# Exponential into two SBUF tiles in turns, token ring one slot shorter

## The chip, the cores and the metric

The kernel runs on one core of a Trainium2 chip. The metric is the time of one execution on the device in microseconds, over all of the kernel's work. Five engines take part, each with its own queue that it works through in order: TensorE (PE in the profile, with its weight loads as PEld), VectorE (DVE), ScalarE (ACT), GpSimd (POOL) and SyncE (SP), which here only issues DMAs. TensorE writes to PSUM alone; VectorE and ScalarE read and write PSUM and SBUF; GpSimd and the DMAs work on SBUF in this kernel.

## The reference

Causal attention with a bias from cumulated positions, and after it a maxout feed-forward on the tokens. There are 8 batches, 8 heads, 576 positions and 64 dimensions a head; the feed-forward goes from 512 to 768 and back to 512.

```python
scores = scale * np.matmul(q, k.transpose(0, 1, 3, 2))
cum = np.cumsum(np.maximum(s, 0.0), axis=-1)
bias = -(cum[:, :, :, None] - cum[:, :, None, :])
scores = np.where(causal, -1000000000.0, scores + np.minimum(bias, 0.0))
scores = scores - np.max(scores, axis=-1, keepdims=True)
attn = np.exp(scores)
attn = attn / (np.sum(attn, axis=-1, keepdims=True) + 1e-09)
x = np.matmul(attn, v)        # then [B, S, H*D] -> [4608, 512]
h = np.maximum(np.maximum(x @ w1, x @ w2), x @ w3)
out = h @ w_out
```

## The kernel before

**Visits and steps.** Heads are worked on in pairs, and a pair's queries in blocks of 128 (the last block has 64). A visit is one pair with some of its blocks. Batches 0 and 1 have two visits a pair, of blocks 0 and 1 and of blocks 2, 3 and 4 (16 visits, 40 steps). Batches 2 to 7 have one visit a pair, of all five blocks: 24 visits, 120 steps, steps 40 to 159. A step is one block for both heads of the pair. Block 0 looks at 128 keys, block 1 at 256, and so on to 512; block 4, with 64 queries of each head stacked on the 128 partitions, looks at all 576. `stacked(v)` (line 118) is true for the visits of five blocks, and `below(t)` (line 114) for their blocks 0 to 3.

**The path of a step.** `scores(t)` (line 362) multiplies on TensorE into a PSUM tile `s` of two banks, one a head; there are two such tiles, in turns. In a visit of five blocks the matmuls are those of lines 379, 390 and 395, and they read two tiles a head, `h` and `l`. `highest(t)` (line 452) masks and takes the smallest of the negated scores on VectorE (line 456), in place in PSUM, with the constant `later` as second input; block 4 has a plain maximum (line 461). `expo(t)` (line 465) takes the exponential on ScalarE with the row sums (line 471), back into the same PSUM tile, and scales the sums (`se`, line 476). `probs(t)` (line 481) takes the reciprocal `ri` (line 494) on VectorE, makes the high half of the probabilities `prh` in 16 bits on ScalarE (line 510), and on VectorE the low half, `prl` = probability minus high half (line 513). Both read the PSUM tile; `prl` reads `prh` as its second input. The halves go through DMA transposes on SyncE's queue (lines 516 and 522) to `ph` and `pl`, which `values` (line 563) multiplies with the values' halves `vh` and `vl` (line 582). `prl` in block 4 has a second instruction of 64 columns; its `prh` counterpart also writes into the tile `prl`.

**The token groups.** `values` gives a slab of tokens `x`, in a high half (ScalarE, line 591) and a low half (VectorE, line 592). The four pairs of a batch and a phase (phase 0: the first 256 positions; phase 1: the other 320) make a set, and `add_set` (line 700) queues its 22 groups: 18 up projections of 12 matmuls (line 714), each evicted by ScalarE (line 728) or VectorE (line 731), with the hidden halves `hh` and `hl` made by GpSimd (lines 720 and 721), and 4 down projections of 18 matmuls (line 756), evicted by ScalarE (line 764) with the scale `os` from GpSimd (line 749). Groups use three PSUM tiles in turns.

**The ring.** The token slabs of the first three pairs of a set's second phase, and of all four pairs of the first phase from batch 2 on, lie in weight tiles that are free by then: `RING` (line 535) names them, and `x_tile` takes the next in turn, 14 times in all. `reserve` (line 537) runs groups of the queue until the set that held that tile has issued its up projections. The tiles `w22` and `w23` hold the last two raw weights; both are decoded by step 17.

**Order.** The schedule is written out by hand: the order of the program is the order on each engine. A step of the loop at line 929 goes

```python
parts = probs(t); next(parts)      # ri, prh
highest(t + 1)
next(parts)                        # prl, transposes
drain(); flush()                   # evictions that are pending, hh and hl
if ready() and cost[0] > 0: run_group()
scores(t + 2)
expo(t + 1)
drain(); flush()
...                                # what the plan has for this step
while ready() and cost[0] > 0: run_group()
values(*due.pop(0))                # where a phase of a visit is complete
```

How many groups run in a step is set by a budget, `cost`: a step earns 4400 ns (4700 from step 60) less what its scores and values cost TensorE, and a group costs 0.417 ns a column and matmul. Among the plan's entries are the preparation of the next visits: the halves of queries and keys (`h` by ScalarE at lines 153 and 157 and by VectorE at line 162, `l` by GpSimd at lines 140 to 146, 166 and 171), the values' halves (ScalarE line 349, VectorE line 354), the decoding of the weights (through tiles with the tag `t`, three of them, line 612) up to step 17, and `later_keys` (line 446) at step 20.

Of the kernel before, what the change touches and what calls it, by code (L numbers as in the profile page):

```python
# [8 lines left out]
F32 = mybir.dt.float32  # L9
F32R = mybir.dt.float32r  # L10
F16 = mybir.dt.float16
BF16 = mybir.dt.bfloat16
I32 = mybir.dt.int32
I64 = mybir.dt.int64
AF = mybir.ActivationFunctionType
# [6 lines left out]
def kernel(  # L22
# [11 lines left out]
    P = 128  # L34
    D = 64
    B, NP, _, QKV = qkv.shape
    HB, S = s.shape
# [8 lines left out]
    Q4 = 4 * P  # L46
# [12 lines left out]
    wpool = ctx.enter_context(tc.tile_pool(name="wpool", bufs=1))  # L59
# [3 lines left out]
    moe = ctx.enter_context(tc.tile_pool(name="moe", bufs=1))  # L63
# [8 lines left out]
    steps = [(v, qb) for v, (_, _, qbs) in enumerate(visits) for qb in qbs]  # L72
# [41 lines left out]
    def below(t):  # L114
        v, qb = steps[t]
        return stacked(v) and qb < 4

    def stacked(v):
        return len(visits[v][2]) == 5
# [65 lines left out]
    def load_w(i, dma=None):  # L185
# [14 lines left out]
        out=tri, in_=tri, pattern=[[-1, P]], compare_op=ALU.is_ge, fill=NEG, base=0, channel_multiplier=1  # L200
    )
    nc.gpsimd.memset(tri4, 0.0)
    for j in range(2):
        r = slice(j * D, (j + 1) * D)
        nc.gpsimd.affine_select(
            out=tri4[r], in_=tri4[r], pattern=[[-1, D]], compare_op=ALU.is_ge, fill=NEG, base=0, channel_multiplier=1
# [153 lines left out]
    U = {}  # L360
# [83 lines left out]
    future = []  # L444

    def later_keys():
        m = wpool.tile([P, Q4], BF16, tag="w23", name="later")
        nc.gpsimd.memset(m[:, 0:Q4 - P], 0.0)
        nc.gpsimd.tensor_copy(out=m[:, Q4 - P:Q4], in_=tri)
        future.append(m)  # L450
# [14 lines left out]
    def expo(t):  # L465
        ps, nm, nk = U[t]
        nj = 2 if nk < S else 1
        sm = small.tile([P, 2], F32, tag="sm", name=f"sm{t}")
        for j in range(nj):
            sc = ps[:, j] if nj == 2 else ps  # L470
            nc.scalar.activation(  # L471
                out=sc, in_=sc, func=AF.Exp, bias=nm[:, j:j + 1], scale=-1.0 if below(t) else 1.0,
                accum_out=sm[:, j:j + 1],
            )
        se = small.tile([P, 2], F32, tag="se", name=f"se{t}")
        nc.scalar.activation(out=se[:, :nj], in_=sm[:, :nj], func=AF.Copy, scale=1.0 / PSC, bias=EPS / PSC)
        SE[t] = (se, nj)
# [54 lines left out]
    taken = [0]  # L532
    done = set()

    RING = [f"w{n}" for n in (10, 11, 12, 13, 14, 15, 16, 17, 22)]

    def reserve(tag, b, ph):
        while owner.get(tag, (b, ph)) not in done | {(b, ph)}:
# [3 lines left out]
    def x_tile(v, ph):  # L542
# [11 lines left out]
        if g == 0:  # L554
            tag = RING[taken[0] % len(RING)]
            taken[0] += 1
# [218 lines left out]
    later = []  # L775
# [85 lines left out]
    for v in range(NP, len(visits)):  # L861
        w = v - NP
# [7 lines left out]
    for f, e in ((prep4, 1), (prep5, 0), (load, 7), (prep2, 4), (prep3, 3)):  # L870
        for v in range(len(visits)):
            t = first[v] - e
            if v % NP == 0 and f in (prep4, prep5):
                t = first[v] + 1 + (f is prep5) if v else -1
# [4 lines left out]
            if f is load and NP <= v < 2 * NP:  # L879
                t = first[v] - 6  # L880
            if 2 * NP * NB - 2 <= v < 2 * NP * NB and f in (load, prep2, prep3):
                t = first[v] - (8 if f is load else 4 if f is prep3 and v % 2 == 0 else 5)
            if stacked(v) and f in (load, prep2, prep3):
                n = v - 2 * NP * NB
# [22 lines left out]
    for i, t in fetched.items():  # L907
        at(t, load_w, i, nc.scalar.dma_start)
    at(1, spread, 1)
    at(20, later_keys)  # L910

    prep2(0)
# [9 lines left out]
    vscale1(scale_of(0))  # L922
    scores(1)
    expo(0)
    for t in sorted(k for k in todo if k < 0):
        for f, a in todo[t]:
            if f not in (prep2, prep3) or a[0] > 1:
                f(*a)
    for t, (v, qb) in enumerate(steps):
# [18 lines left out]
        if t + 1 < len(steps):  # L948
            expo(t + 1)
# [73 lines left out]
```

## Time and profile before

| | |
|---|---|
| three runs | 895.49, 897.57, 898.87 us; median 897.57 |
| profiled execution | span 895.1 us from the first to the last instruction; no other time of it is given |
| TensorE matmuls | busy 818.6 us, 91% of the span |
| VectorE | 599.0 us, 67% |
| ScalarE | 569.4 us, 64% |
| GpSimd | 347.9 us, 39% |
| mean granted TensorE clock | 0.964 |

The profile is of one execution. A row of grouped instructions reads: line, engine, operation, what it writes and reads, shapes, count, then the busy time of the group in us and the mean of one in ns, then the idle time of the engine before them and what ended it. A row of waits reads: engine and what it wrote, what it waited for, then the us in total, how many times, and the longest. In the timeline a row has the start, the duration, the instructions, and in brackets the idle time before. Names of tiles are given without their numbers, so `s` is the scores' tile of any step.

### The profile page before, as it was taken

Reading aid. Unit: us, or ns where it says so; the run is one execution under the profiler, and the core shown is the slowest. Engines: PE = TensorE matmul, PEld = TensorE weight load, DVE = VectorE, ACT = ScalarE, POOL = GpSimd, SP = SyncE. Lnnn points to the kernel's source line nnn. Section 1 sums busy time; section 2 is a strip of 40 time slices with the busy share of each in tenths; the row PEclk is TensorE's granted clock in tenths of the full one; section 3 lists DMA queues with packets and bytes.
Section 4 is the critical chain, followed back from the end, with each engine's and each line's share of the span. In section 5 each row is a group of like instructions: output and inputs, shape, how many; then the busy total and the mean of one; then the engine's idle time right before and its main releaser. Section 6 shows DMA issues by size and latency. Waiting matters only on the chain.

```text
span 895.1 us, 19807 instructions
## 1 busy us (share of the span) xinstructions
PE 818.6 (91%) x7000; PEld 641.1 (72%) x7000; DVE 599.0 (67%) x1504; ACT 569.4 (64%) x1502; POOL 347.9 (39%) x553
## 2 busy tenths in 40 slices
PE   3567769998999989999999999999999999999998
PEld 2445657776667768777787778777787788777875
DVE  6898886666777767676666767676767667663110
ACT  4668567676677677766666776767667676754111
POOL 4111322223444535454454545445454436421211
PEclk9856889999999999999999999999999999999999
DMA  8972446676778676857767676866657777534000
GB/s 297 284 189 60 95 96 142 142 147 141 183 166 174 144 169 127 141 134 147 137 154 159 103 172 141 160 140 139 139 146 147 144 149 129 116 74 85 13 13 30
DMA packets 240243, 122.32 MB, mean 137 GB/s; under 512 B 216016, under 2 KB 224720, under 8 KB 240144
## 3 DMA queue, kind: packets, MB, share of 16 engines
q1 hardware_dynamic: 236112, 108.73, 57.4%
q10 hardware_dynamic: 4032, 12.32, 4.1%
q8 instruction: 55, 0.90, 0.5%
q14 instruction: 44, 0.36, 0.2%
HBM read 60.18 MB, written 9.44 MB: 78 GB/s over the span
## 4 chain that ended last, share of the span: by engine, by line
PE 63%; DVE 3%; ACT 3%; POOL 2%; issue 1%; DMA 1%; SPq 0%; DVEq 0%; POOLq 0%; ACTq 0%
PE pm L714 36%; PE po L756 13%; PE s L379 6%; PE av L582 6%; PE s L390 2%; DVE prl L513 1%; ACT prh L510 1%; ACT s L471 1%; DVE m L731 1%; POOL hh L720 1%; DMA raw<-in_qk_dram 1%; POOL l L171 0%; POOL hl L721 0%; DVE h L162 0%; DVE s L456 0%
## 5 line engine op out<-in xcount | busy, mean ns | idle before, releaser
L714 PE MATMUL pm<-x,w 128*128 128x256 f16 (+1 forms) x3456 | 453.5, 288 | 3.8 <-DVE x L592 2.1
L714 PEld LDWEIGHTS <-w 128*128 128x128 f16 x3456 | 329.7, 98 | 94.4 <-issue 8.4
L720 POOL CAST hh<-m 128x256 f16<-128x256 f32 (+1 forms) x96 | 55.3, 576 | 356.7 <-DVE m L731 299.3
L510 ACT ACTIVATE prh<-s,ri 128x512 f16<-128x512 f32 (+3 forms) x288 | 142.1, 539 | 81.0 <-DVE ri L494 76.4
L513 DVE SCALAR_TENSOR_TENSOR prl<-s,ri,prh 128x512 f16<-128x512 f32 (+3 forms) x288 | 152.9, 568 | 47.4 <-ACT prh L510 29.0
L731 DVE SCALAR_TENSOR_TENSOR m<-pm,m 128x256 f32<-128x256 f32 (+1 forms) x192 | 87.3, 455 | 125.2 <-PE pm L714 100.7
L471 ACT ACTIVATE s<-s,nm 128x512 f32<-128x512 f32 (+4 forms) x288 | 151.2, 525 | 12.6 <-DVE nm L456 5.6
L756 PE MATMUL po<-hh,w 128*128 128x256 f16 (+1 forms) x768 | 149.9, 287 | 0.0
L756 PEld LDWEIGHTS <-w 128*128 128x128 f16 x1152 | 110.1, 98 | 33.4 <-issue 4.8
L456 DVE CUSTOM_DVE_ANT_0 s<-s,later 128x128 f32<-128x128 f32 (+1 forms) x192 | 94.7, 493 | 33.5 <-PE s L379 30.2
L756 PE MATMUL po<-hl,w 128*128 128x320 f16 (+1 forms) x384 | 110.1, 287 | 1.5 <-POOL hl L721 1.4
L728 ACT ACTIVATE m<-pm 128x256 f32<-128x256 f32 (+1 forms) x96 | 39.1, 407 | 93.9 <-PE pm L714 89.5
L721 POOL TENSOR_TENSOR hl<-m,hh 128x256 f16<-128x256 f32 (+1 forms) x96 | 75.4, 785 | 7.8
L171 POOL TENSOR_TENSOR l<-raw,h 64x576 fp32r<-64x576 f32 x48 | 67.2, 1400 | 12.5 <-ACT h L157 11.1
L764 ACT ACTIVATE o<-po,os 128x256 f32<-128x256 f32 (+1 forms) x64 | 31.9, 499 | 62.0 <-PE po L756 53.2
L461 DVE TENSOR_REDUCE nm<-s 128x1 f32<-128x576 f32 (+3 forms) x64 | 49.9, 780 | 22.0 <-PE s L395 12.4
L140 POOL CAST l<-kb 64x576 fp32r<-64x576 f32 x48 | 32.2, 671 | 72.8 <-PE s L390 71.5
L582 PEld LDWEIGHTS <-vh 128*64 128x64 f16 x832 | 45.9, 113 | 19.0 <-issue 13.1
L379 PE MATMUL s<-h 128*128 128x128 f32 (+1 forms) x192 | 54.0, 363 | 4.2 <-DVE prl L513 1.7
L471 ACT ACTIVATION_READ_ACCUMULATOR s<-s,nm 128x1 f32 x288 | 57.3, 199 | 0.0
L591 ACT ACTIVATE x<-av 128x256 f16<-128x256 f32 (+1 forms) x64 | 26.2, 410 | 41.1 <-PE av L582 39.9
L582 PE MATMUL av<-ph,vh 128*64 128x320 f16 (+3 forms) x384 | 51.9, 290 | 0.0
(139 smaller groups left out, 1086.6 us busy)
## 6 DMA issues: line engine op xcount, KB each, us to landing
raw<-in_qk_dram SPq DMA_DIRECT2D x48, 608.0 KB, 4.7
r<-in_w_dram ACTq DMA_DIRECT2D x20, 512.0 KB, 4.9
rv<-in_qkv_dram SPq DMA_DIRECT2D x32, 320.0 KB, 3.3
out_dram<-o SPq DMA_DIRECT2D x32, 160.0 KB, 2.0
out_dram<-o SPq DMA_DIRECT2D x32, 128.0 KB, 2.0
raw<-in_qkv_dram SPq DMA_DIRECT2D x8, 480.0 KB, 3.9
ph<-prh SPq DMA_TRANSPOSE x192, 3.3
pl<-prl SPq DMA_TRANSPOSE x192, 2.9
```

Source lines behind the costliest of these rows:

```text
L171: nc.gpsimd.tensor_tensor(out=l[far, QP:V0], in0=raw[far, QP:V0], in1=h[far, QP:V0].bitcast(F32), op=ALU.subtract)
L379: nc.tensor.matmul(ps[:, j, :nk], lhsT=w[:, qs], rhs=w[:, QP:QP + nk], start=(x == "h"), stop=(x == "l"), skip_group_check=True,)
L456: nc.vector.tensor_tensor_reduce(out=sc[:, j], in0=sc[:, j], in1=future[0][:, Q4 - nk:Q4], scale=-1.0, scalar=3.0e38, op0=ALU.add, op1=ALU ...
L471: nc.scalar.activation(out=sc, in_=sc, func=AF.Exp, bias=nm[:, j:j + 1], scale=-1.0 if below(t) else 1.0, accum_out=sm[:, j:j + 1],)
L510: nc.scalar.activation(out=hi, in_=src, func=AF.Copy, scale=sc)
L513: nc.vector.scalar_tensor_tensor(out=lo, in0=src, scalar=sc, in1=hi, op0=ALU.mult, op1=ALU.subtract)
L582: nc.tensor.matmul(av[j * D:(j + 1) * D, c0:nq], lhsT=lt, rhs=rt, start=(n < 2), stop=(n >= len(todo) - 2), skip_group_check=True,)
L714: nc.tensor.matmul(pm[:, :nq], lhsT=w[:, wt, kt, :], rhs=xt, start=(n == 0), stop=(n == 3 * NKT - 1))
L720: nc.gpsimd.tensor_copy(out=st["hh"][:, ft, :nq], in_=m1[:, :nq])
L721: nc.gpsimd.tensor_tensor(out=st["hl"][:, ft, :nq], in0=m1[:, :nq], in1=st["hh"][:, ft, :nq], op=ALU.subtract)
L731: nc.vector.scalar_tensor_tensor(out=m1[:, :nq], in0=pm[:, :nq], scalar=HSC, in1=m1[:, :nq], op0=ALU.mult, op1=ALU.max)
L756: nc.tensor.matmul(pm[:, :nq], lhsT=W[18 + ft][:, wt, dt, :], rhs=st[ht][:, ft, :nq], start=(n == 0), stop=(n == 3 * NFT - 1),)
```

## The change

In visits of five blocks `expo` writes the exponential to an SBUF tile `e` of 32 bits instead of back to PSUM, in `w22` and `w23` in turns, and `probs` reads it from there. The row sums are taken as before. `w22` leaves the ring, which has eight slots then instead of nine. `later` moves from `w23` to a tile with the tag `t`.

```diff
     def later_keys():
-        m = wpool.tile([P, Q4], BF16, tag="w23", name="later")
+        m = moe.tile([P, Q4], BF16, tag="t", name="later", bufs=3)
@@ expo
         sm = small.tile([P, 2], F32, tag="sm", name=f"sm{t}")
+        e = ps
+        if stacked(steps[t][0]):
+            e = wpool.tile([P, 2 * Q4], F32, tag=f"w{22 + t % 2}", name=f"e{t}")
+            e = e[:, 0:2 * nk].rearrange("p (j n) -> p j n", j=2) if nj == 2 else e[:, 0:S]
+            U[t] = (e, nm, nk)
         for j in range(nj):
-            sc = ps[:, j] if nj == 2 else ps
+            sc, so = (ps[:, j], e[:, j]) if nj == 2 else (ps, e)
             nc.scalar.activation(
-                out=sc, in_=sc, func=AF.Exp, bias=nm[:, j:j + 1], scale=-1.0 if below(t) else 1.0,
+                out=so, in_=sc, func=AF.Exp, bias=nm[:, j:j + 1], scale=-1.0 if below(t) else 1.0,
                 accum_out=sm[:, j:j + 1],
             )
@@
-    RING = [f"w{n}" for n in (10, 11, 12, 13, 14, 15, 16, 17, 22)]
+    RING = [f"w{n}" for n in (10, 11, 12, 13, 14, 15, 16, 17)]
```

## The prediction

> **What bounds the kernel now.** I read the totals first, then the span cut at 250 and 800 us, then TensorE's waits in the middle part.
>
> ```profile
> PE 818.6 (91%) x7000; PEld 641.1 (72%) x7000; DVE 599.0 (67%) x1504; ACT 569.4 (64%) x1502; POOL 347.9 (39%) x553
> ```
>
> ```profile
> core 0: us, PE busy (x) PEld busy (x) DVE busy (x) ACT busy (x) POOL busy (x), PEclk, DMA share, GB/s
> 0.00:250.00 250.00, 189.78 (x1597) 147.36 (x1598) 195.93 (x427) 166.14 (x427) 71.58 (x115) 0.88 0.65 162
> 250.00:800.00 550.00, 537.77 (x4648) 422.74 (x4647) 382.46 (x1029) 382.73 (x1028) 259.60 (x409) 1.00 0.69 143
> 800.00:895.10 95.10, 91.03 (x759) 70.95 (x757) 20.66 (x49) 20.49 (x49) 16.68 (x31) 1.00 0.16 36
> ```
>
> The visits of five query blocks lie in the middle part. There TensorE is busy 537.8 of 550 us at full clock, so 12.2 us is all that an edit of its waiting can win. The first 250 us hold 60 us of idle TensorE, but there `e` is still the PSUM buffer; the last 95 us are token groups. Both stay as they are. In the middle part these waits end TensorE's idle time:
>
> ```profile
> PE s L390 <- DVE prl L513: 4.9, 4, 2.7
> PE pm L714 <- DVE x L592: 2.1, 2, 1.2
> PE s L379 <- ACT se L476: 1.3, 1, 1.3
> PE po L756 <- POOL hl L721: 0.9, 2, 0.5
> PE s L379 <- DVE prl L513: 0.8, 1, 0.8
> PE s L379 <- POOL l L171: 0.7, 2, 0.4
> PE s L379 <- ACT m L728: 0.7, 1, 0.7
> ```
>
> Four of the seven rows wait before `scores`, the cases that the edit is about. Two of these name ScalarE, and the timeline shows one such wait next to an undisputed one:
>
> ```profile
> 371.34 0.20 ACT L476 ACTIVATE se<-sm 128x2 f32<-128x2 f32 x1
> 372.40 1.80 PE L714 MATMUL pm<-x,w 128*128 128x320 f16 x12
> 374.00 1.14 DVE L513 SCALAR_TENSOR_TENSOR prl<-s,ri,prh 128x384 f16<-128x384 f32 x2
> 375.29 0.47 PE L390 MATMUL s<-h 128*128 128x256 f32 x2 [1.08 <-DVE prl L513]
> ...
> 627.13 0.28 DVE L513 SCALAR_TENSOR_TENSOR prl<-s,ri,prl 128x64 f16<-128x64 f32 x1
> 627.55 0.47 PE L379 MATMUL s<-h 128*128 128x256 f32 x2 [1.32 <-ACT se L476]
> ```
>
> Both score matmuls start 0.14 to 0.15 us after the `prl` of two steps earlier ended (374.00 + 1.14, and 627.13 + 0.28). I therefore count the two ScalarE rows as waits for the slot too: 4.9 + 1.3 + 0.8 + 0.7 = **7.7 us**.
>
> **The slot (gain).** `scores(t+2)` refills the PSUM slot of step t. After the change its last reader is the exponential of step t, not `prl`. At 375 us that exponential and its sums were over at 371.34, before the token group ended at 372.40 + 1.80 = 374.20; the wait of 1.08 us would be gone. So would the others, except the longest, 2.7 us at 325:
>
> ```profile
> 322.05 4.69 DMA raw<-in_qk_dram
> ...
> 330.16 0.34 DVE x L592
> ...
> 330.54 0.38 PE pm L714 x2
> ```
>
> ```profile
> 325.00:330.00 5.00, 4.50 (x31) 3.78 (x32) 2.94 (x6) 3.95 (x10) 2.76 (x5) 0.68 1.00 227
> ```
>
> Here the chain of waits runs through a load that lands at 326.74, then through ScalarE's and VectorE's queues to the token tile `x` at 330.5, for which TensorE waits again. Scores that start 2.7 us earlier only lengthen that second wait. I count this wait at no gain (bounds 0 and 2.7). Around it the granted clock is 0.68 over 5 us, 0.32 x 5 = 1.6 us of lost matmul speed, now under the wait. If idle time moves to just before 330.5, the slow stretch may follow it into work that TensorE is late with: a loss between 0 and 1.6, and I take the middle, 0.8. The gain is 7.7 - 2.7 = 5.0 us.
>
> **ScalarE and VectorE, undisturbed.** The new placements are not in the trace; these rows are nearest.
>
> ```profile
> L471 ACT ACTIVATE s<-s,nm 128x512 f32<-128x512 f32 x46 | 30.4, 661 | 4.0 <-DVE nm L456 3.2
> L510 ACT ACTIVATE prh<-s,ri 128x512 f16<-128x512 f32 x69 | 44.6, 680 | 11.9 <-DVE ri L494 11.9
> L510 ACT ACTIVATE prh<-s,ri 128x128 f16<-128x128 f32 x46 | 14.3, 363 | 11.8 <-DVE ri L494 11.8
> L349 ACT ACTIVATE vh<-rv,inv 128x640 f16<-128x640 f32 x24 | 19.6, 818 | 2.1 <-DVE inv L310 2.1
> L513 DVE SCALAR_TENSOR_TENSOR prl<-s,ri,prh 128x512 f16<-128x512 f32 x69 | 49.7, 748 | 24.3 <-ACT prh L510 15.2 <-ACT prl L510 9.1
> L513 DVE SCALAR_TENSOR_TENSOR prl<-s,ri,prh 128x384 f16<-128x384 f32 x46 | 26.2, 611 | 0.8 <-ACT prh L510 0.8
> ```
>
> PSUM to PSUM takes 661 ns and PSUM to SBUF 680, so an exponential into SBUF costs 0 to 20 ns more; I take 20. `prh` grows by (680 - 363)/384 = 0.83 ns an element, 786 at 640; from SBUF the `vh` row has 818, so +32. The 24 visits have 216 exponentials and 240 reads: 216 x 20 ns + 240 x 32 ns = 12 us on ScalarE. It is idle 550 - 382.7 = 167 us of this part, and TensorE's 7.7 us of slot waits no longer hang on it, so I price this at nothing. Uncovered it is 0.5 us a visit, 12 us. On VectorE `prl` grows by (748 - 611)/128 = 1.07 ns an element, 885 at 640. The same operation with both inputs in SBUF, `vl`, has a median of 876 (below). Undisturbed nothing changes; bounds -9 ns and 0 each.
>
> **VectorE against GpSimd (loss).** That median has a tail:
>
> ```profile
> L354 DVE SCALAR_TENSOR_TENSOR vl<-rv,inv,vh x36: 470/876/1281, 81.5 to 798.8; 128x640 f16<-128x640 f32 x32, 128x256 f16<-128x256 f32 x4
> L513 DVE SCALAR_TENSOR_TENSOR prl<-s,ri,prh x288: 334/609/753, 18.5 to 815.6; 128x512 f16<-128x512 f32 x48, 128x128 f16<-128x128 f32 x32, 128x256 f16<-128x256 f32 x32, 128x384 f16<-128x384 f32 x32
> ```
>
> ```profile
> 362.56 1.40 POOL L171 TENSOR_TENSOR l<-raw,h 64x576 fp32r<-64x576 f32 x1
> 362.84 0.60 DVE L513 SCALAR_TENSOR_TENSOR prl<-s,ri,prh 128x128 f16<-128x128 f32 x2
> 363.36 1.28 DVE L354 SCALAR_TENSOR_TENSOR vl<-rv,inv,vh 128x640 f16<-128x640 f32 x1
> 364.06 0.74 POOL L749 TENSOR_SCALAR os<-p,kw 128x1 f32<-128x1 f32 x1
> ```
>
> ```profile
> L171 POOL TENSOR_TENSOR l<-raw,h 64x576 fp32r<-64x576 f32 x46 | 64.4, 1400 | 9.6 <-ACT h L157 8.2
> L166 POOL CAST l<-h 64x640 fp32r<-64x640 f32 x45 | 34.3, 761 | 7.4 <-ACT h L153 5.5
> ```
>
> No `prl` of 288 was held up (longest 753 ns); the two at 362.84 ran inside GpSimd's `l`. The `vl` that began in that same `l`, 0.60 us before its end, took 1.28 instead of 0.88 us, and the tiny `os` behind it took 0.74 us. What differs is that `vl` reads both inputs from SBUF. After the change every `prl` of a five-block visit does. The Trainium skill, page "SBUF — State Buffer", section "Who interferes with whom", states this rule, and it speaks against the change: a VectorE instruction with two SBUF inputs and a GpSimd instruction that reads SBUF hold a shared port in turn, each for its whole length. The trace agrees with the turns; by the rule's full blocking the `vl` would have lost 0.60 us, and it lost 0.40.
>
> The price: GpSimd is busy 259.6/550 = 47% of the time, so about 0.47 x 240 = 113 `prl` start inside one of its operations. A quarter of that time is `l` (64.4/259.6), with half of 1.4 us left on average, the rest operations of some 0.7 us with half left: 0.25 x 0.70 + 0.75 x 0.35 = 0.44 us. That is 50 us if all of it is lost, and 113 x (0.44 - 0.20) = 27 us with the 0.20 us that the `vl` got back. I take 38 us, 1.6 us a visit; VectorE goes from 382.5/550 = 70% to about 76%. Behind a held `prl` queue the evictions of token groups, `x`, `qlo` and the next maximum.
>
> ```profile
> DVE m L731 <- PE pm L714: 39.6, 51, 2.1
> DVE s L456 <- PE s L379: 29.8, 33, 2.3
> DVE nm L461 <- PE s L395: 10.0, 14, 1.5
> ```
>
> VectorE itself waits 79 us for TensorE in this part, and TensorE never waits for `m`: most of the 38 us lies in that. What passes through shows in the waits that stay, `x`, `hl` and `l`: 2.1 + 0.9 + 0.7 = 3.7 us at a load of 70%. Scaled as load over idle, (0.76/0.24)/(0.70/0.30) = 1.36, they grow by 1.3 us; with GpSimd's own holds, such as `os` above, I take 1.5. Bounds: 0, and all 38 us.
>
> **Ring and `later`: nothing.** The 14 slabs come in a fixed order, and by the planner's own costs (4700 ns a step) the ninth is taken at step 103, while the set whose slot it takes, batch 0's second phase, issued its last up projection at step 40. No group is forced earlier, so TensorE's order stays. `later` keeps its two GpSimd operations of step 20 and moves to a slot whose last weight was decoded at step 13. No DMA is added or moved. The two `e` slots alternate, and `prl` of step t-2 precedes the maximum of step t on VectorE, so they add no wait.
>
> **Sum.** -5.0 + 0.8 + 1.5 = -2.7 us on a span of 895.1: 892.4. The profile gives no time for that execution beside its span; the median of the runs, 897.57, is 2.5 us above it, and I keep the distance: **894.9 us**.
>
> **Rivals.**
> *The whole wait is won.* All 7.7 us go, nothing of VectorE's lateness reaches TensorE: 897.6 - 7.7 = 889.9. For it: VectorE's 79 us of waiting. Against: the `x` wait at 330.5.
> *The port decides (slower).* `prl` meets the 1.4 us `l`, two to a visit, and the groups of TensorE run out of their three PSUM buffers behind it. It decides once the cover in a visit falls short of the 1.6 us by a third. If 0.5 us a visit passes, 24 x 0.5 = 12 us: 897.6 - 5.0 + 0.8 + 12 = 905.4. For it: 25 to 30% of VectorE free is little for engines that issue in order. Against: no `m` wait now. By the Trainium skill's page named above it would be somewhat likelier, since full blocking gives 50 us instead of 38.
> *Nothing arrives.* `l` of the second head ends just before the first scores of a visit (two waits, 0.7 us), so scores freed of `prl` meet `l`, `hl` or `x` instead: 897.6. That the edit doesn't free the slot comes to the same time; the readers of PSUM in the diff speak against it.
>
> **Chances.** Forecast 0.42, whole gain 0.26, port 0.18, nothing 0.14. A measurement of this kernel tells about 0.5%, 4.5 us, from no change: faster means below 893.1, slower above 902.1. The forecast's own spread, 891 to 899, gives 0.06 of its 0.42 to faster; the whole gain gives 0.24, the port 0.16 to slower, the forecast 0.02. That is faster 0.30, same 0.52, slower 0.18. The range of 8 in 10 reaches from 888.5, just past the whole gain, to 904.0, most of the way to the port.
>
> **What would show it.** Right: no wait of scores for `prl` after 250 us; `prl` at 128x512 with a mean of 0.85 to 1.0 us and a maximum near 2; exponentials near 680 ns; `l` and `os` with longer tails; TensorE busy some 540 of 550 us. Wrong: `prl` still at 748 (no port), `m` among TensorE's waits with several us (the port decides), or a changed order of token groups.

## The result, and the profile after

The changed kernel takes **903.41 us** (median of ten runs, 899.92 to 908.22) against 896.66 us for the kernel before: a ratio of **1.007** with a 95% interval of 1.005 to 1.009. It is slower by 0.7%, where no measurable change was the likeliest forecast and 894.9 us its number.

The totals of the profiled execution after, and its middle part:

```profile
span 901.0 us, 19664 instructions
...
PE 817.5 (91%) x7000; PEld 642.0 (71%) x7000; DVE 638.8 (71%) x1504; ACT 567.2 (63%) x1502; POOL 373.6 (41%) x553
```

```profile
250.00:800.00 550.00, 532.42 (x4606) 420.46 (x4605) 418.22 (x1016) 377.20 (x1016) 285.37 (x407) 0.99 0.68 142
```

The span grew by 901.0 - 895.1 = 5.9 us. TensorE's work is the same (817.5 us busy against 818.6), but in the middle part it idles 550 - 532.4 = 17.6 us instead of 12.2. VectorE is busier by 418.2 - 382.5 = 35.8 us there (39.8 over the whole span), GpSimd by 285.4 - 259.6 = 25.8 us; ScalarE isn't. What ends TensorE's idle time in the same part, after:

```profile
PE s L379 <- POOL l L171: 10.3, 12, 2.5
PE av L587 <- DMA ph<-prh: 4.9, 2, 3.9
PE po L761 <- POOL hl L726: 0.9, 2, 0.5
PE pm L719 <- DVE x L597: 0.6, 1, 0.6
```

Every wait of scores for the PSUM slot is gone in this part, 7.7 us. In their place stand 10.3 us for `l` from GpSimd, where there were 0.7, and 4.9 us for the transposed `ph`; the wait for `x` fell from 2.1 to 0.6. That makes -7.7 + 9.6 + 4.9 - 1.5 = +5.3 us, nearly the 5.4 us more of idle time.

The low half of the probabilities, the forms of five-block visits first (`<-e`), then the others (`<-s`); durations are minimum, median and maximum in ns:

```profile
L518 DVE SCALAR_TENSOR_TENSOR prl<-e,ri,prh x216: 337/615/1973, 246.8 to 820.8; 128x512 f16<-128x512 f32 x36, 128x128 f16<-128x128 f32 x24, 128x256 f16<-128x256 f32 x24, 128x384 f16<-128x384 f32 x24
...
L518 DVE SCALAR_TENSOR_TENSOR prl<-s,ri,prh x72: 335/608/751, 18.9 to 240.9; 128x512 f16<-128x512 f32 x24, 128x128 f16<-128x128 f32 x16, 128x256 f16<-128x256 f32 x16, 128x384 f16<-128x384 f32 x16
```

In one kernel stand both placements: with both inputs in SBUF the longest takes 1973 ns, with one in PSUM 751; in the kernel before, where all have one in PSUM, none took more than 753. One of the two longest waits of scores, in the timeline after (start, duration, instruction, idle time before it and what ended it):

```profile
352.32 1.82 DVE L518 SCALAR_TENSOR_TENSOR prl<-e,ri,prh 128x512 f16<-128x512 f32 x2
352.41 1.19 POOL L140 CAST l<-kb 64x576 fp32r<-64x576 f32 x1
...
353.55 1.07 POOL L141 CAST l<-qr 64x512 fp32r<-64x512 f32 x1
353.82 0.42 PE L379 MATMUL s<-h 128*128 128x128 f32 x2
...
354.73 0.82 DVE L162 SCALAR_TENSOR_TENSOR h<-raw,h 64x640 fp32r<-64x640 f32 x1
354.84 1.97 POOL L171 TENSOR_TENSOR l<-raw,h 64x576 fp32r<-64x576 f32 x1
...
356.87 0.33 PE L379 MATMUL s<-l 128*128 128x128 f32 x1 [2.52 <-POOL l L171]
```

The two `prl` and GpSimd's copies of lines 140 and 141 take turns: 1.82 instead of some 1.4 us, 1.19 instead of 0.67, 1.07 instead of 0.63. These copies are bias rows for the next visit. Behind them in GpSimd's queue is line 171, the last piece of `l` for the scores that are due now. It starts late, is held again by `qlo` (line 162), takes 1.97 instead of 1.40 us, and TensorE waits 2.52 us. The same place in the kernel before:

```profile
353.77 1.40 POOL L171 TENSOR_TENSOR l<-raw,h 64x576 fp32r<-64x576 f32 x1
...
354.35 0.41 PE L379 MATMUL s<-h 128*128 128x128 f32 x2
...
355.22 0.33 PE L379 MATMUL s<-l 128*128 128x128 f32 x1 [0.36 <-POOL l L171]
```

There `l` was ready at 353.77 + 1.40 = 355.17 us, after the change at 354.84 + 1.97 = 356.81, 1.6 us later: line 171 started 1.07 us later and took 0.57 us longer. The scores began 0.5 us earlier (353.82 against 354.35). So of the 2.2 us by which this wait grew, 1.6 are the late `l`.

### The profile page after: what moved, and what is told of

Read it like the earlier page. It is cut to its first block, busy times and chain, and to the rows that moved or that the text cites. A ratio compares the mean times of both kernels' runs of the same rounds, so it can differ in the third digit from the quotient of the medians.

```text
span 901.0 us, 19664 instructions
## 1 busy us (share of the span) xinstructions
PE 817.5 (91%) x7000; PEld 642.0 (71%) x7000; DVE 638.8 (71%) x1504; ACT 567.2 (63%) x1502; POOL 373.6 (41%) x553
## 4 chain that ended last, share of the span: by engine, by line
PE 51%; POOL 9%; issue 6%; DVE 4%; DMA 2%; ACT 1%; SPq 0%; POOLq 0%; ACTq 0%; DVEq 0%
PE pm L719 33%; PE po L761 8%; PE s L379 4%; PE av L587 4%; POOL l L171 3%; POOL l L141 2%; POOL l L140 1%; DMA ph<-prh 1%; DVE m L736 1%; DVE prl L518 1%; POOL hh L725 1%; PE s L390 1%; POOL l L146 1%; POOL hl L726 1%; DVE h L162 1%
## 5 line engine op out<-in xcount | busy, mean ns | idle before, releaser
L518 DVE SCALAR_TENSOR_TENSOR prl<-e,ri,prh 128x512 f16<-128x512 f32 (+3 forms) x216 | 147.9, 720 | 15.0 <-ACT prh L515 9.5
L515 ACT ACTIVATE prh<-e,ri 128x512 f16<-128x512 f32 (+3 forms) x216 | 114.0, 570 | 57.6 <-DVE ri L499 55.3
L476 ACT ACTIVATE e<-s,nm 128x128 f32<-128x128 f32 (+4 forms) x216 | 116.4, 545 | 4.7 <-DVE nm L456 4.6
L171 POOL TENSOR_TENSOR l<-raw,h 64x576 fp32r<-64x576 f32 x48 | 73.4, 1530 | 8.4 <-ACT h L157 7.0
L726 POOL TENSOR_TENSOR hl<-m,hh 128x256 f16<-128x256 f32 (+1 forms) x96 | 73.5, 766 | 7.8
L379 PE MATMUL s<-l 128*128 128x128 f32 (+1 forms) x192 | 49.3, 326 | 10.5 <-POOL l L171 10.3
L515 ACT ACTIVATE prh<-s,ri 128x512 f16<-128x512 f32 (+3 forms) x72 | 35.6, 540 | 33.5 <-DVE ri L499 29.8
```

The lines of the kernel that those rows point to most:

```text
L171: nc.gpsimd.tensor_tensor(out=l[far, QP:V0], in0=raw[far, QP:V0], in1=h[far, QP:V0].bitcast(F32), op=ALU.subtract)
L379: nc.tensor.matmul(ps[:, j, :nk], lhsT=w[:, qs], rhs=w[:, QP:QP + nk], start=(x == "h"), stop=(x == "l"), skip_group_check=True,)
L476: nc.scalar.activation(out=so, in_=sc, func=AF.Exp, bias=nm[:, j:j + 1], scale=-1.0 if below(t) else 1.0, accum_out=sm[:, j:j + 1],)
L515: nc.scalar.activation(out=hi, in_=src, func=AF.Copy, scale=sc)
L518: nc.vector.scalar_tensor_tensor(out=lo, in0=src, scalar=sc, in1=hi, op0=ALU.mult, op1=ALU.subtract)
L726: nc.gpsimd.tensor_tensor(out=st["hl"][:, ft, :nq], in0=m1[:, :nq], in1=st["hh"][:, ft, :nq], op=ALU.subtract)
```

## Experiments

Two theories stood after this. *Turns:* VectorE and GpSimd take turns at SBUF, GpSimd falls behind, and the piece of `l` that is last in its queue is what reaches TensorE. *ScalarE:* its slower accesses to SBUF, 12 us in the prediction, carry the loss. The ring or the constant as cause, and an order that is worth something whatever the exponential's place, were tried beside them.

**The ring and the constant alone.**

```diff
+        m = moe.tile([P, Q4], BF16, tag="t", name="later", bufs=3)
...
+    RING = [f"w{n}" for n in (10, 11, 12, 13, 14, 15, 16, 17)]
```

`expo` stays as in the kernel before.

> The ring of eight slots and the moved constant alone; the exponential stays in PSUM. If the loss comes from VectorE and GpSimd taking turns at SBUF, or from ScalarE's slower accesses to SBUF, this is the kernel before: 896.7 us within 2. If the ring or the constant is the cause, it is near 903.

Measured: 897.02 us, ratio 1.0001 (0.9987 to 1.0016). These two parts cost nothing.

**The late piece first on GpSimd, in the changed kernel.**

```diff
-                        at(o + (1 if n == 0 else 2), head_klo, v, j)
+                        todo.setdefault(o + (1 if n == 0 else 2), []).insert(0 if n else 99, (head_klo, (v, j)))
```

> The changed kernel, with one order on GpSimd's queue turned round: the last piece of l (line 171) ahead of the next visit's bias rows (lines 140 to 146), which stand before it in the same step. If turns at SBUF make GpSimd late and scores wait for l, the 10.3 us of waits for l and the half-clock stretch of 1.7 us behind one of them go: 903.4 - 12 = 891 us, with prl still near 940 ns at 128x512. If ScalarE's slower exponential and prh are the cause, or the wait for the transposed ph at 327 us, nothing of that depends on this order: 902 to 904.

Measured: **890.91 us**, ratio to the kernel before 0.9931 (0.9914 to 0.9948). TensorE's waits in the middle part, and two rows of groups (busy us, mean ns):

```profile
PE av L587 <- DMA ph<-prh: 4.8, 1, 4.8
PE gmv L283 <- DVE ambv L279: 1.9, 2, 1.6
PE po L761 <- POOL hl L726: 1.0, 3, 0.5
PE pm L719 <- DVE x L597: 0.6, 1, 0.6
...
PE pm L719 <- DVE m L736: 0.2, 1, 0.2
```

```profile
L518 DVE SCALAR_TENSOR_TENSOR prl<-e,ri,prh 128x512 f16<-128x512 f32 x69 | 65.6, 978 | 14.0 <-ACT prh L515 9.7
L171 POOL TENSOR_TENSOR l<-raw,h 64x576 fp32r<-64x576 f32 x45 | 65.5, 1456 | 37.2 <-ACT h L157 35.9
```

No wait for `l` is left, though `prl` is held no less (978 ns against 942) and ScalarE does what it did. Line 171 now waits 35.9 us for its input, where it used to wait in the queue. So the whole loss went with this one turn of GpSimd's order, 12.5 us in all, and ScalarE's slower accesses cost nothing that shows.

**The same order in the kernel before.** The edit is the same line.

> The same turn of order in the kernel before. It has 0.7 us of waits for l, so the turns theory expects 896 within 1.5 us, no change. If the order is worth something by itself, whatever the exponential's place, this gains as much as the same edit in the changed kernel.

Measured: 895.38 us, ratio 0.9981 (0.9966 to 0.9995): 1.2 us less by the medians and at most 3 by the interval, against 12.5 us in the changed kernel. Most of what the order is worth there comes from the change. With this order in both kernels the change wins 895.38 - 890.91 = 4.5 us, near the 5.0 us that the prediction counted for the slot.

**The slot held until `prl`.**

```diff
+            HELD[t] = ps[:, 0, 0:1] if nj == 2 else ps[:, 0:1]
...
+        if t in HELD:
+            hold = small.tile([P, 1], F32, tag="hold", name=f"hold{t}")
+            nc.vector.tensor_copy(out=hold, in_=HELD.pop(t))
```

The copy stands behind `prl` and reads one column of the PSUM tile.

> The changed kernel with the PSUM slot held until prl again, by a copy of one column from it on VectorE behind prl (120 copies, some 0.1 us each): the cost of the SBUF accesses without the gain of the free slot. The turns theory expects the waits of scores for VectorE back, 7.7 us and more since prl is later by up to 0.2 us at 128x512, and the waits for l shorter, since scores come later: 906 to 916 us. If the free slot brings nothing in the changed kernel, it stays at 903 to 904.

Measured: 908.47 us, ratio 1.0134 (1.0111 to 1.0158), 5.1 us above the changed kernel. Its waits:

```profile
PE s L379 <- POOL l L171: 7.6, 15, 1.4
PE s L390 <- DVE hold L523: 6.3, 6, 2.8
PE s L379 <- DVE ri L501: 1.9, 1, 1.9
```

The slot waits are back (6.3 us for the copy behind `prl` alone) and those for `l` are shorter, 7.6 us. So the waits for `l` are not only scores that come earlier: with the slot held until after `prl` they can't come earlier than in the kernel before, and they still wait 7.6 us for `l`, against 0.7 there. Freeing the slot is worth something in the changed kernel too; how much of the 5.1 us is that and how much the copies themselves, 147 ns each in the profile, is open.

**The second input of `prl` from PSUM.**

```diff
-            nc.vector.scalar_tensor_tensor(out=lo, in0=src, scalar=sc, in1=hi, op0=ALU.mult, op1=ALU.subtract)
...
+        last = ALU.subtract if not stacked(v) else ALU.min if below(t) else ALU.max
...
+            nc.vector.scalar_tensor_tensor(out=lo, in0=src, scalar=sc, in1=second, op0=ALU.mult, op1=last)
```

In five-block visits `second` is the scores' PSUM tile. This kernel leaves out the subtraction of `prh` there, so it doesn't compute the low half of the probabilities.

> The changed kernel, but prl of five-block visits takes its second input from the PSUM tile of the scores instead of prh (as a minimum or maximum; the subtraction of prh is left out, so the low half of the probabilities is not computed). Every prl then has one SBUF input, and the PSUM slot is held until prl as before the change; ScalarE's exponential into SBUF and prh from SBUF stay. If the turns of VectorE and GpSimd carry the loss, prl is back at 748 ns for 128x512 with no tail, l at 1400 ns, and the time is that of the kernel before, 896.6 us within 3; against the run that holds the slot (908.5) it is 12 us less. If ScalarE's accesses to SBUF carry it, up to their 12 us remain: 903 to 909.

Measured: 891.87 us, ratio 0.9953 (0.9933 to 0.9973), 16.6 us less than with the slot held and both inputs in SBUF.

```profile
L528 DVE SCALAR_TENSOR_TENSOR prl<-e,ri,s 128x512 f16<-128x512 f32 x69 | 49.2, 740 | 0.7 <-DMA pl<-prl 0.7
...
L478 ACT ACTIVATE e<-s,nm 128x512 f32<-128x512 f32 x46 | 31.1, 682 | 3.0 <-DVE nm L456 2.9
...
L140 POOL CAST l<-kb 64x576 fp32r<-64x576 f32 x44 | 29.6, 672 | 72.5 <-PE s L390 71.3
```

`prl` is at 740 ns, GpSimd's copy at 672, as in the kernel before, while the exponential into SBUF keeps its 682 ns. With one input in PSUM the turns are gone, and with them the loss. That it came out 5 us below the kernel before, where 896.6 within 3 was expected, is probably a side effect of the experiment, which no run shows by itself: this `prl` no longer waits for `prh` (VectorE's idle time before it is 0.7 us, 24.3 in the kernel before), so the slot can be free earlier. The 16.6 us are therefore not the turns alone: the copies and that wait are in them.

**A smaller budget before the gap at 325 us.** At that place the changed kernel waited 3.9 us for `ph`, and 4.8 us with the late piece first.

```diff
-        cost[0] = min(cost[0] + (4400.0 if t < 60 else STEP_NS) - pe_cost(t), 4000.0)
+        cost[0] = min(cost[0] + (4000.0 if 44 <= t < 60 else 4400.0 if t < 60 else STEP_NS) - pe_cost(t), 4000.0)
```

> The changed kernel with the last piece of l ahead of the bias rows (890.9 us), and a smaller budget of token groups, 4000 instead of 4400 ns, in steps 44 to 59. If the wait at 325 to 330 us, 4.8 us for ph and a half-clock stretch behind it, is there because the queue of token groups has run empty (by the planner's costs in steps 56 and 57), a few groups kept for those steps remove it: 885 to 888 us. If it is the transposes themselves that are late, it stays: 891.

Measured: **886.08 us**, ratio 0.9881 (0.9861 to 0.9901), the fastest kernel of this study. The stretches around the place, columns as in the prediction:

```profile
320.00:325.00 5.00, 5.00 (x45) 3.87 (x44) 4.35 (x10) 4.84 (x12) 3.06 (x6) 1.00 1.18 267
325.00:330.00 5.00, 5.00 (x45) 4.32 (x42) 4.82 (x12) 4.75 (x15) 1.95 (x2) 1.00 0.90 196
```

TensorE has no gap there and the full clock. The wait was an empty queue of token groups, not late transposes.

> The same smaller budget in the kernel before. Its waits in that place are 2.7 us for the slot and 0.9 us for x, with the half-clock stretch. If they too come from the empty queue, the time falls by 2 to 4 us from 896.6; if the slot wait of 2.7 us is one like the other slot waits, it stays, and nothing changes beyond 1 us.

Measured, in the kernel before: 895.00 us, ratio 0.9975 (0.9962 to 0.9989), 1.9 us less, at the edge of the 2 to 4 expected of an empty queue. From 325 to 330 us TensorE has no gap here either, and the full clock; its waits for the slot at other places stay:

```profile
325.00:330.00 5.00, 5.00 (x48) 3.84 (x47) 3.75 (x8) 4.44 (x11) 3.65 (x7) 1.00 0.69 147
...
PE s L379 <- DVE prl L513: 2.9, 5, 0.9
PE s L390 <- DVE prl L513: 2.3, 4, 0.8
```

## Why the prediction was wrong

**Right: the waits counted.** All 7.7 us of slot waits were as read, the two that named ScalarE among them: none is left after the change.

**Right in its price: the wait at 325 us brings nothing.** It was left out of the gain since TensorE would only wait further on. It did, for `ph` instead of `x`: 3.94 us after, 2.7 + 0.9 before.

```profile
327.05 0.43 PE L587 MATMUL av<-ph,vh 128*64 128x256 f16 x2 [3.94 <-DMA ph<-prh]
```

What the reading of that place left out is why TensorE had nothing else to do. It named a late load; with some token groups kept for these steps the gap is gone in both kernels.

The half-clock stretch moved with it as feared (clock 0.66 from 325 to 330 us), and a second one came behind the wait shown above (0.73 from 355 to 360), which the prediction had not.

```profile
325.00:330.00 5.00, 2.95 (x21) 2.19 (x22) 3.65 (x7) 3.59 (x9) 2.11 (x3) 0.66 0.95 164
355.00:360.00 5.00, 3.13 (x17) 2.26 (x18) 2.57 (x9) 0.96 (x2) 2.53 (x2) 0.73 0.82 206
```

**Right: the prices of single operations.** The exponential was put at 680 ns and took 682; `prh` was put 32 ns up and went from 680 to 713. `prl` at 128x512 was expected at 0.85 to 1.0 us with a maximum near 2, and has 942 ns and 1.97 us:

```profile
L518 DVE SCALAR_TENSOR_TENSOR prl<-e,ri,prh 128x512 f16<-128x512 f32 x69 | 63.2, 942 | 11.5 <-ACT prh L515 7.0
L515 ACT ACTIVATE prh<-e,ri 128x512 f16<-128x512 f32 x69 | 47.0, 713 | 20.7 <-DVE ri L499 18.6 <-DMA ph<-prh 1.8
L476 ACT ACTIVATE e<-s,nm 128x512 f32<-128x512 f32 x46 | 31.1, 682 | 2.9 <-DVE nm L456 2.7
```

VectorE's load was put at +38 us and 76%, and rose by 35.8 us to 418.2/550 = 76%; some 7 us of the rise is not `prl` but `qlo`, which has a mean of 1024 ns instead of 876, 45 times.

**Right: that ring, constant and ScalarE cost nothing that shows.** The ring and the constant by their own run; ScalarE by the runs with the late piece first and with the second input from PSUM, both faster than before although ScalarE's accesses stayed.

**Wrong: what passes through to TensorE.** The failing step is "with GpSimd's own holds, such as `os` above, I take 1.5". The price of the turns was worked out for VectorE alone, and the pass-through was scaled with VectorE's load. But a turn can hold up either side: GpSimd's busy time rose by 25.8 us, beside VectorE's 35.8, and that had no term of its own. The 0.7 us of waits for `l` that were scaled by 1.36 became 10.3, because line 171 stands last in GpSimd's queue, behind 1.5 us of bias rows that nobody needs yet (2.4 us in the timeline above, 352.41 to 354.84), and had nothing to spare at two visits even before. So one term, put at 1.5 us, was 9.6 us for `l` alone, plus a half-clock stretch behind one of those waits (0.27 x 5 = 1.4 us by the row of 355 us above). With the late piece moved forward the 891 us expected of it came out at 890.91. That the measured time still lies in the range, 888.5 to 904.0, is no merit of this sum: its upper end was drawn toward the port rival.

**The rivals.** "The port decides" had the right cause and sign and a time 2 us from the result, 905.4, but the wrong place: it expected token groups to run out of PSUM buffers, and in the middle part no wait for `m` appeared. "Nothing arrives" had the right place, `l` of the second head, and the wrong size. Neither joined the two. "The whole wait is won" had the 7.7 us right and took the pass-through for nothing. The page "SBUF — State Buffer" of the Trainium skill, section "Who interferes with whom", says that the second to issue is the one that blocks, whichever engine it is; the rows at 352 to 356 us show both cases within four microseconds.

## What to carry to other kernels

When an edit moves an operand from PSUM to SBUF, count the SBUF inputs of the instruction that reads it: at two, VectorE and GpSimd held each other up here, and both sides need a price. Then look at what is last in the held engine's queue before a deadline; a late piece behind work that isn't due yet turns microseconds of load into waits of the bound engine, and moving it forward cost nothing here. A freed buffer is worth only what isn't waiting right behind it: the change lost 0.7% by itself and won 0.7% with one line of order, 1.2% with the queue kept filled as well. The order alone won 0.2% in the kernel before, the budget alone 0.25%; both together were not run there.

## What the runs showed of the hardware

Undisturbed, VectorE's multiply and subtract takes about as long with its first input from SBUF as from PSUM. In the rows of line 518 above, which have the same mix of shapes, minimum and median are 337 and 615 ns from `e`, 335 and 608 from `s`; the maxima, 1973 and 751, are what differs.

The 2.52 us that TensorE waited up to 356.87 were followed by a stretch at a clock of 0.73. The other long wait for `l` in the same run, 2.54 us, was not:

```profile
651.85 0.33 PE L379 MATMUL s<-l 128*128 128x128 f32 x1 [2.54 <-POOL l L171]
```

```profile
650.00:655.00 5.00, 3.15 (x29) 2.84 (x30) 2.46 (x9) 1.05 (x3) 3.20 (x4) 1.00 0.94 212
655.00:660.00 5.00, 5.00 (x48) 4.50 (x46) 2.90 (x10) 3.28 (x12) 2.41 (x4) 1.00 0.43 76
```

So the length of a wait alone doesn't tell whether the clock drops; what else decides was not tried.
